# Twelve query feature maps by two ScalarE passes, three groups of spread reciprocals copied out of PSUM, and new instruction orders

## The chip, the cores and the metric

The kernel runs on one core of one Trainium2 chip. The metric is the device time of one execution in microseconds (us). A core has five engines, each with its own queue of instructions worked off in order: TensorE (PE in the profile; PEld is its weight load), VectorE (DVE), ScalarE (ACT), GpSimd (POOL) and SyncE (SP, which here issues DMAs). They are tied together by semaphores alone. TensorE writes to PSUM, which has eight banks; VectorE and ScalarE read it.

## The reference

Four residual layers on one sequence of 2,048 tokens and 512 features, in the order A, B, A, B with the same weights for both A layers and for both B layers. Each has 32 heads of 16 features. A is linear attention, B is attention in a sliding window of 256 keys.

```python
# layer A, after a layer norm of x (without gain or bias)
phi = lambda t: jnp.where(t > 0, t + 1, jnp.exp(t)) + 1e-6
pq, pk = phi(q), phi(k)
kv = jnp.einsum("bhsd,bhse->bhde", pk, v)
z = jnp.einsum("bhsd->bhd", pk)
num = jnp.einsum("bhqd,bhde->bhqe", pq, kv)
den = jnp.einsum("bhqd,bhd->bhq", pq, z)[..., None] + 1e-6
o = num / den                                 # then o @ wo, added to x

# layer B, after a layer norm of x
scores = jnp.einsum("bhqd,bhkd->bhqk", q, k) * (Dh ** -0.5)
mask = (idx[:, None] - idx[None, :] >= 0) & (idx[:, None] - idx[None, :] < 256)
p = _softmax(jnp.where(mask, scores, -1e9))
o = jnp.einsum("bhqk,bhkd->bhqd", p, v)       # then o @ wo, added to x
```

## The kernel before, in words

The sequence is cut into 16 tiles of 128 tokens. Everything stays in on-chip memory; x is loaded once and the result written once.

The program is not written engine by engine. `Plan` records every operation as a node of a graph, with its engine or a choice of engines, what it reads and writes and which PSUM banks it needs. A compressed table at the end of the file (`TABLE`) then gives three things: the order of all operations, the engine of each operation that has a choice, and the PSUM bank of each tile. `place` reads the table, `synchronise` derives the waits on semaphores, and each engine plays its operations in the table's order. So the table decides which instruction stands behind which on every engine.

The work has these stages. The first A layer: for each tile a layer norm (`norm`: statistics on VectorE, the inverse root on GpSimd, the scaling on VectorE), a transpose, the key product (`a_k`) with its feature map, the Gram sums of normed x against mapped keys ("g", line 475, 128 x 512 matmuls in four banks), and the query product (`a_q`, `feat`, line 414) with its feature map.

The feature map is `phi`. ScalarE takes the exponential out of PSUM into a buffer tE (line 423), VectorE clamps it to 1 and adds 1e-6 (line 424), and VectorE takes the maximum of that and the product in PSUM plus 1 + 1e-6 (line 425).

Then comes a barrier (`barrier`, lines 517 to 557), since linear attention needs the sums over all keys: kv is masked to blocks and multiplied into the output weights, giving M (four 512-column matmuls, line 521, each copied out of PSUM, "Me", line 389). For each group of four tiles the denominators are made on TensorE ("den", line 537), inverted by VectorE in float32 (line 541), cast to bf16 by either engine ("recb", line 542) and spread over the head features by TensorE into four banks ("spread", line 550). VectorE multiplies the mapped queries by each bank (line 557). Tiles of later groups pass the barrier later, inside the next stage.

The B layer (`middle`): for each tile the output of the A layer (`a_out`, added to x on line 568), a layer norm, query, key and value products (`b_qkv`, `b_v`), and then, for a block of 128 queries at a time, scores (`b_scores`, line 634), their exponentials on ScalarE (line 644), the causal mask on VectorE (line 652), scores and exponentials of the far end of the window (`b_far`, lines 723 and 732) with a mask on GpSimd or VectorE (lines 703 and 704), the product with the values (`b_values`, line 753), the division (lines 765 and 766) and the output product and residual (`b_out`). Keys are copied from PSUM ("bke", lines 585 and 586) and then put in a layout with zeros by two DMAs for each tile ("kd", on SP's queue); values likewise ("bve", "vd").

While the first B layer runs, the key products, value products ("ve", line 389) and some query products of the second A layer are already made for the tiles that are finished. The second barrier and the second B layer follow. In the two B layers ScalarE's exponentials of scores run nearly without a break; I call these the exponential stages.

Beside TensorE's own work there are 10 + 6 matmuls without use ("fill", lines 270 and 275).

## Time and profile before

| | |
|---|---|
| median of 3 runs | 412.48 us (412.22 to 414.48) |
| the profiled execution's own time | 412.48 us |
| its span, first to last instruction | 410.8 us |
| mean granted TensorE clock | 0.998 |
| busy: TensorE, VectorE, ScalarE, GpSimd | 389.5, 344.4, 341.9, 126.3 us |
| first exponential of scores of the first B layer | 62.75 us |
| first exponential of scores of the second B layer | 259.02 us |

Times inside the profile are microseconds from the start of the span. A group of instructions is given as line, engine, operation, output from input, shapes and count, then its busy time and the mean nanoseconds of one, then the engine's idle time just before them and what ended it. "idle before <- X" is a wait that X ended. The chain of waits is followed back from the last instruction: each piece is what the next one waited for, or the instruction before it on its engine. A stretch in which the chain stays on one engine is a stretch in which that engine did not wait.

### The profile page before, as it was taken

The numbers are of one execution on the slowest core, as the hardware profiler recorded it, in microseconds if no ns is written. First come the engines' busy times: TensorE is split into PE (matmuls) and PEld (weight loads), VectorE is DVE, ScalarE is ACT, GpSimd is POOL, SyncE is SP. The second block draws the span as 40 slices with busy tenths as digits, with TensorE's granted clock in tenths as the row PEclk, the third lists the DMA queues.
The fourth block names the chain that finished last, engine by engine and source line by source line (L and its number), as shares of the span: only waits on it lengthen the run. The fifth ranks groups of instructions, "written<-read, shape, count | busy, mean of one in ns | idle before, by whom it ended". The sixth has DMA issues, their size and how long they took to land.

```text
span 410.8 us, 17457 instructions
## 1 busy us (share of the span) xinstructions
PE 389.5 (95%) x7639; PEld 260.5 (63%) x7715; DVE 344.4 (84%) x803; ACT 341.9 (83%) x428; POOL 126.3 (31%) x221
## 2 busy tenths in 40 slices
PE   8999999999999999999999999999999989899996
PEld 4645676766475576565566767586757745566674
DVE  5998899989989899778887879997899778766675
ACT  2633559998999999999998255999999999999992
POOL 3665761122251253231401113112234024431310
PEclk9999999999999999999999999999999999999999
DMA  7934117542234624343212100443324333352442
GB/s 246 240 66 96 61 41 146 141 123 56 67 82 98 117 77 95 83 118 83 69 44 53 29 2 14 106 122 81 93 67 104 87 80 94 81 147 67 135 115 61
DMA packets 67460, 37.84 MB, mean 92 GB/s; under 512 B 48248, under 2 KB 62456, under 8 KB 67384
## 3 DMA queue, kind: packets, MB, share of 16 engines
q1 hardware_dynamic: 66896, 35.41, 35.6%
q8 instruction: 61, 1.00, 1.0%
q0 software_dynamic: 480, 1.31, 1.0%
q14 instruction: 15, 0.12, 0.1%
q10 hardware_dynamic: 8, 0.00, 0.0%
HBM read 6.29 MB, written 2.10 MB: 20 GB/s over the span
## 4 chain that ended last, share of the span: by engine, by line
PE 60%; ACT 26%; DVE 10%; issue 2%; DMA 1%; POOL 0%; DVEq 0%; POOLq 0%; SPq 0%
PE ps L400 21%; ACT pb L644 16%; PE ps L414 14%; PE ps L753 8%; PE ps L634 5%; ACT pb L732 4%; PE ps L475 3%; ACT vp L644 3%; DVE XQ L557 2%; ACT tE L423 1%; PE ps L723 1%; DVE xres L568 1%; DMA kB<-vp 1%; PE ps L1007 1%; PE ps L451 1%
## 5 line engine op out<-in xcount | busy, mean ns | idle before, releaser
L644 ACT ACTIVATE pb<-ps 128x1024 bf16<-128x1024 f32 (+2 forms) x224 | 206.8, 1022 | 6.3 <-PE ps L634 5.2
L753 PEld LDWEIGHTS ps<-vB,pb 128*128 128x128 bf16 x2560 | 77.7, 96 | 12.9 <-issue 3.7
L753 PE MATMUL ps<-vB,pb 128*128 128x34 bf16 x2560 | 83.8, 177 | 0.6 <-ACT pb L644 0.4
L414 PE MATMUL ps<-xT,wBp 128*128 128x128 bf16 x1024 | 69.1, 219 | 0.7 <-DVE stats L361 0.4
L423 ACT ACTIVATE tE<-ps 128x512 bf16<-128x512 f32 x64 | 38.4, 613 | 34.4 <-PE ps L400 14.7
L414 PEld LDWEIGHTS ps<-xT,wBp 128*128 128x128 bf16 x1024 | 59.1, 98 | 12.2 <-issue 4.4
L703 POOL TENSOR_SCALAR_AFFINE_SELECT pb<-pb 128x1024 bf16<-128x1024 bf16 x33 | 37.8, 1145 | 82.6 <-ACT pb L732 30.1
L363 POOL TENSOR_SCALAR ve<-mv 128x1 f32<-128x1 f32 x64 | 15.6, 243 | 142.6 <-DVE mv L362 140.3
L634 PE MATMUL ps<-XQ,kB 32*128 32x256 bf16 (+2 forms) x1024 | 49.6, 268 | 3.3 <-ACT vp L644 0.9
L568 DVE TENSOR_TENSOR xres<-ps,xres 128x512 bf16<-128x512 f32 x63 | 43.1, 684 | 8.8 <-PE ps L400 8.2
L400 PE MATMUL ps<-wA,XQ 128*128 128x512 bf16 x172 | 45.8, 379 | 2.1 <-issue 1.0
L361 DVE BATCH_NORM_STATS2 stats<-xres 128x6 f32<-128x512 bf16 x64 | 43.4, 682 | 2.4 <-DMA xres<-in_A_x_dram 2.0
L652 DVE TENSOR_TENSOR pb<-pb,tri 128x512 bf16<-128x512 bf16 (+1 forms) x112 | 43.2, 398 | 2.2 <-ACT pb L644 2.1
L732 ACT ACTIVATE pb<-ps 128x1024 bf16<-128x1024 f32 x42 | 41.5, 1065 | 0.6 <-PE ps L723 0.4
L364 POOL TENSOR_TENSOR rs<-ve,negh 128x1 f32<-128x1 f32 x64 | 36.9, 577 | 5.3
L414 PE MATMUL ps<-XQ,wA 128*128 128x128 bf16 x512 | 35.5, 219 | 0.0
L634 PEld LDWEIGHTS ps<-XQ,kB 32*128 32x128 bf16 x1024 | 15.5, 92 | 31.5 <-ACT pb L644 7.5
L414 PEld LDWEIGHTS ps<-XQ,wA 128*128 128x128 bf16 x512 | 30.7, 98 | 6.0 <-ACT pb L644 0.8
L400 PE MATMUL ps<-M,XQ 128*128 128x512 bf16 x113 | 30.9, 380 | 2.6 <-issue 1.0
L400 PE MATMUL ps<-wBv,xT 128*128 128x512 bf16 x111 | 31.1, 380 | 1.9 <-issue 1.1
L400 PE MATMUL ps<-wBo,oT 128*128 128x512 bf16 x107 | 29.7, 380 | 2.0 <-issue 0.6
L644 ACT ACTIVATE vp<-ps 128x1024 bf16<-128x1024 f32 (+2 forms) x32 | 26.6, 925 | 1.8 <-PE ps L634 1.8
(115 smaller groups left out, 530.6 us busy)
## 6 DMA issues: line engine op xcount, KB each, us to landing
vB<-vS SPq DMA_DIRECT2D x64, 136.0 KB, 2.6
kB<-vp SPq DMA_DIRECT2D x64, 128.0 KB, 2.1
wA<-in_A_wqkv_dram SPq DMA_DIRECT2D x3, 512.0 KB, 6.1
out_dram<-xres POOLq DMA_DIRECT2D x10, 128.0 KB, 2.1
xres<-in_A_x_dram SPq DMA_DIRECT2D x2, 512.0 KB, 5.2
pb<-in_B_wqkv_dram SPq DMA_DIRECT2D x1, 1024.0 KB, 7.1
xres<-in_A_x_dram SPq DMA_DIRECT2D x3, 256.0 KB, 5.0
out_dram<-xres SPq DMA_DIRECT2D x5, 128.0 KB, 2.2
```

The lines of the kernel that those rows point to most:

```text
L361: self.on("DVE", "stats", lambda e: e.bn_stats(K.stats[:, t, :], K.xres[:, t, :]), key, dve(512), rd=[("xres", t)], wr=[("stats", t)])
L364: self.pow = self.on("POOL", "pow", lambda e: e.tensor_tensor(K.rs[:, t, :], K.ve[:, t, :], K.negh[:], ALU.pow), key + 0.03, (640, 690), r ...
L400: m = e.matmul(K.ps(ps), lhs(c), rhs(c), start=c == 0, stop=c == 3)
L414: m = e.matmul(K.ps(ps)[:, f * P:(f + 1) * P], w(c, f), xT(c), start=c == 0, stop=c == 3)
L423: self.on("ACT", "E", lambda e: e.activation(K.tE[:, s, :], K.ps(ps), ACT.Exp, bias=0.0), key, act(512), wr=[("tE", s)], ps=[ps])
L568: self.on("DVE", "res", lambda e: e.tensor_tensor(K.xres[:, t, :], K.ps(po), K.xres[:, t, :], ALU.add), key, dve(512), rd=[("xres", t)], w ...
L634: m = e.matmul(K.ps(ps[gq])[:, ns * i:ns * i + ns], K.kB[rows, j % 4, 2 * f + b, :, :], K.XQ[rows, f, q:q + ns], start=True, stop=True, ti ...
L644: return e.activation(out(2 * h, 2, ns), i, ACT.Exp, bias=0.0, scale=0.25)
L652: return e.tensor_tensor(x, x, K.tri[:, 0, sh:64].unsqueeze(1).unsqueeze(1).to_broadcast([P, 4, n, 64 - sh]), ALU.mult)
L703: return e.affine_select(out=x, in_=x, compare_op=ALU.is_ge, fill=0.0, base=-2, pattern=[[0, 16], [-2, 64]], channel_multiplier=1)
L732: return e.activation(far(h), i, ACT.Exp, bias=0.0, scale=0.25)
L753: m = e.matmul(K.ps(ps)[:, 34 * u:34 * u + 34], K.P((b // 2) % rp)[:, gq, f, o:o + P], K.vB[:, (b // 2) % 4, b % 2, r, :], start=i == 0, s ...
```

## The change

Seven query tiles of the first A layer (0 to 6) and five of the second (4 to 8) get another form of the last step of the feature map: ScalarE reads the product out of PSUM a second time and writes it, plus 1 + 1e-6, in bf16 to the place of the mapped query; VectorE then takes the maximum of two bf16 tiles in on-chip memory, in place of the maximum that reads PSUM. For group 0 in the first barrier and groups 0 and 1 in the second, the spread reciprocals are first copied out of PSUM in bf16, by ScalarE or VectorE as the table says, into tE, and VectorE multiplies two bf16 tiles. The reciprocal is written in bf16 directly, and the cast "recb" is gone. The keys of tile 0 are written from PSUM straight into kB by two copies with a factor of 0 or 1 for each row (`par2`, made by a small reduction), and the copy and the two DMAs of that tile are gone. The first scores of each B layer are cut by query tile: `b_first` makes the 128 x 128 scores of query tile 0, then of tile 1, in place of two `b_scores` of 256 queries for two head groups each. The paths under `whole` and `po` are in the code but are switched off (`WHOLE` is empty and `FIRST` 0). The table is new: all orders, engine choices and banks.

By the orders of the two programs, ScalarE has seven of the copies of spread reciprocals and VectorE five. Of the operations with a choice some others change engine: M copies 8 and 0 (ScalarE, VectorE) to 6 and 2; value products 8 and 8 to 2 and 14; vS copies 7 and 25 to 9 and 23; key copies 8 and 24 to 5 and 25. Two far masks go from GpSimd to VectorE.

```diff
 LONG = ("mf", "zero", "wp", "c6", "c9", "c10", "c14", "c21", "c24")
-SHORT = ("xn", "mk", "md", "ma", "mf", "E1", "recb")
+SHORT = ("xn", "mk", "md", "ma", "mf", "E1", "mx", "pm")
...
+WHOLE = {2: (), 3: ()}
+FIRST = {2: 0, 3: 0}
+BY_ACT = {2: (0, 1, 2, 3, 4, 5, 6), 3: (4, 5, 6, 7, 8)}
+COPIED = {2: (0,), 3: (0, 1)}
+PART = (2, 3)
+NEAR = (0,)
...
+        pool("c2c", zero(lambda: K.one, 1.0 + 1e-6), key + 2, 100, wr=[("one",)])
...
+        self.on("DVE", "par", lambda e: e.tensor_reduce(K.par2[:], K.ident[:].rearrange("p (n a) -> p a n", a=2), mybir.AxisListType.X, ALU.add), 150, dve(128), rd=[("ident",)], wr=[("par",)], after=after)
...
-    def phi(self, ps, out, wr, key, ring):
+    def phi(self, ps, out, wr, key, ring, near=False):
...
         self.on("ACT", "E", lambda e: e.activation(K.tE[:, s, :], K.ps(ps), ACT.Exp, bias=0.0), key, act(512), wr=[("tE", s)], ps=[ps])
+        if near:
+            self.on("ACT", "R", lambda e: e.activation(out(), view(K.ps(ps)), ACT.Identity, bias=K.one[:]), key + 0.005, act(512), rd=[("one",)], wr=wr, ps=[ps])
         self.on("DVE", "E1", lambda e: e.tensor_scalar(K.tE[:, s, :], K.tE[:, s, :], 1.0, 1e-6, op0=ALU.min, op1=ALU.add), key + 0.01, dve(512, "4x"), rd=[("tE", s)], wr=[("tE", s)])
-        self.on("DVE", "phi", lambda e: e.scalar_tensor_tensor(out(), K.ps(ps) if len(out().shape) == 2 else K.ps(ps).rearrange("p (f n) -> p f n", f=4), 1.0 + 1e-6, K.tE[:, s, :] if len(out().shape) == 2 else K.tE[:, s, :].rearrange("p (f n) -> p f n", f=4), ALU.add, ALU.max), key + 0.02, dve(512), rd=[("tE", s)], wr=wr, ps=[ps])
+        if near:
+            self.on("DVE", "mx", lambda e: e.tensor_tensor(out(), out(), view(K.tE[:, s, :]), ALU.max), key + 0.02, dve(512, "2x"), rd=[("tE", s)], wr=wr)
+        else:
+            self.on("DVE", "phi", lambda e: e.scalar_tensor_tensor(out(), view(K.ps(ps)), 1.0 + 1e-6, view(K.tE[:, s, :]), ALU.add, ALU.max), key + 0.02, dve(512), rd=[("tE", s)], wr=wr, ps=[ps])
...
-            self.on("DVE", "rec", lambda e, G=G, ps=ps: e.reciprocal(K.recf[:], K.ps(ps)[:, 0:P]), k + 0.1, dve(128, "recip"), wr=[("recf",)], ps=[ps])
-            self.g.add("recb", {"ACT": act(128), "DVE": dve(128, "2x")}, lambda e, eng, G=G: e.activation(K.rec[:, G, :], K.recf[:], ACT.Copy) if eng == "ACT" else e.tensor_copy(K.rec[:, G, :], K.recf[:]), k + 0.1, rd=[("recf",)], wr=[("rec", G)])
+            def inverse(e, G=G, ps=ps):
+                with K.nc.allow_low_precision(reason="one rounding, to the type that the product reads"):
+                    return e.reciprocal(K.rec[:, G, :], K.ps(ps)[:, 0:P])
+
+            self.on("DVE", "rec", inverse, k + 0.1, dve(128, "recip"), wr=[("rec", G)], ps=[ps])
...
+                if G in COPIED[ph + 1]:
+                    sl = tg % 2
+                    self.copy("sc", bc[tg], lambda sl=sl: K.tE[:, sl, :], lambda b=bc[tg]: K.ps(b), k + 0.25 + 0.01 * tg, 512, wr=[("tE", sl)])
+                    self.on("DVE", "pm", lambda e, x=x, sl=sl: e.tensor_tensor(x(), K.tE[:, sl, :].rearrange("p (f n) -> p f n", f=4), x(), ALU.mult), k + 0.3 + 0.01 * tg, dve(512, "2x"), rd=[("XQ", t), ("tE", sl)], wr=[("XQ", t)])
+                    continue
                 self.on("DVE", "pqd", lambda e, x=x, b=bc[tg]: e.tensor_tensor(x(), K.ps(b).rearrange("p (f n) -> p f n", f=4), x(), ALU.mult), k + 0.3 + 0.01 * tg, dve(512), rd=[("XQ", t)], wr=[("XQ", t)], ps=[bc[tg]])
...
+        if t in NEAR:
+            for a in range(2):
+                o, i = lambda a=a: K.kB[:, r, :, :, a], lambda: K.ps(pk).rearrange("p (b n) -> p b n", b=8)
+                self.either("kz", lambda e, eng, a=a, o=o, i=i: e.activation(o(), i(), ACT.Copy, scale=K.par2[:, a:a + 1]) if eng == "ACT" else
+                            e.tensor_scalar(o(), i(), K.par2[:, a:a + 1], None, op0=ALU.mult), key + 0.05, 512, rd=[("par",)], wr=[("kB", r, a)], ps=[pk])
+            return
...
+    def b_first(self, p, key):
...
+        ps = [Tile(1, "S") for _ in range(4)]
+
+        def put(e):
+            m = None
+            for f in range(4):
+                for gq in range(4):
+                    rows = slice(32 * gq, 32 * gq + 32)
+                    m = e.matmul(K.ps(ps[gq])[:, P * f:P * f + P], K.kB[rows, 0, 2 * f, :, :], K.XQ[rows, f, P * p:P * p + P], start=True, stop=True, tile_position=(32 * gq, 0))
+            return m
+
+        self.pe("s", put, key, 1, 512, mode=(32, 128), occ=237, rd=[("kB", 0, 0), ("kB", 0, 1), ("XQ", p)], ps=ps)
+        for h in range(2):
...
+            self.on("ACT", "ex", ex, key + 0.01 * h, act(1024), wr=[("P", 0, f, 0, h + 3 * p) for f in range(4)], rd=[("P", 0, f) for f in range(4)], ps=two)
+        if p == 0:
+            x = lambda: bass_view(K.P(0)[:, 0, 0, 0:64], [[704, 16], [1, 64]])
+            self.on("DVE", "md", lambda e: e.tensor_tensor(x(), x(), K.tri[:, 0, :].unsqueeze(1).to_broadcast([P, 16, 64]), ALU.mult), key + 0.02, dve(1024, "2x"),
+                    rd=[("P", 0, f, 0, h) for f in range(4) for h in range(2)] + [("tri",)], wr=[("P", 0, f, 0, 2) for f in range(4)])
...
-                    if f % wide[b] == 0:
+                    if j + b == 0 and ph in PART:
+                        if f < 2:
+                            self.b_first(f, base + 0.25 * f)
+                    elif f % wide[b] == 0:
                         self.b_scores(j, b, list(range(f, f + wide[b])), base + j + (f + b) / 4)
```

More of the change, by code (lines that the diff above doesn't have):

```diff
@@ L366, in norm @@
         self.transpose("T", xn, out, [name], wr, key + 0.05, by_pe)
+        if po:
+            self.copy("xe", po, lambda: K.xres[:, t, :], lambda: K.ps(po), key + 0.06, 512, wr=[("xres", t)])
     def transpose(self, name, src, out, rd, wr, key, by_pe):
@@ L389, in copy, with tok @@
         return self.either(name, lambda e, eng: e.activation(out(), src(), ACT.Copy) if eng == "ACT" else e.tensor_copy(out(), src()), key, n, rd=rd, wr=wr, ps=[ps])
-    def tok(self, name, t, lhs, rhs, rd, key):
+    def tok(self, name, t, lhs, rhs, rd, key, whole=False):
         K = self
         ps = Tile(1, K.cls)
+        if whole:
+            self.pe("id", lambda e: e.matmul(K.ps(ps), K.ident[:], K.xres[:, t, :], start=True, stop=False), key - 0.01, 1, 512, rd=[("xres", t), ("ident",)], ps=[ps])
         for h in range(2):
@@ L399, in put @@
                 for c in (2 * h, 2 * h + 1):
-                    m = e.matmul(K.ps(ps), lhs(c), rhs(c), start=c == 0, stop=c == 3)
+                    m = e.matmul(K.ps(ps), lhs(c), rhs(c), start=c == 0 and not whole, stop=c == 3)
                 return m
@@ L757, in b_values @@
                 rd += [("P", i % K.rp, f)] + [("vB", i % 4, a, b) for a in range(2) for b in range(2)]
-                rd += [("P", i % K.rp, f, b, h_) for h_ in range(3) for b in (0, 1)]
+                rd += [("P", i % K.rp, f, b, h_) for h_ in range(5) for b in (0, 1)]
             rd += [("A", i % K.rp) for i in range(max(0, j - 2), j + 1)]
@@ L769, in b_values, with b_out @@
             key + 0.03, dve(256), rd=[("rc", s, h)], wr=[("o", s, h)], ps=[ps])
-    def b_out(self, j, key, by_pe):
+    def b_out(self, j, key, by_pe, whole=False):
         K = self
@@ L865, in middle @@
                 continue
-            self.b_out(j, k, tail)
+            po = self.b_out(j, k, tail, j in WHOLE[ph])
             if last:
```

158 lines of the change are left out of this document (88 added, 70 removed).

## The prediction

> **What bounds the kernel now.** I read the page's busy shares and chain first, then the busy time of each engine by stage, then the chain of waits inside the two stretches in which ScalarE is not full, and last the groups and ScalarE's own timeline. Page first.
>
> ```profile
> PE 389.5 (95%) x7639; PEld 260.5 (63%) x7715; DVE 344.4 (84%) x803; ACT 341.9 (83%) x428; POOL 126.3 (31%) x221
> PE 60%; ACT 26%; DVE 10%; issue 2%; DMA 1%; POOL 0%; DVEq 0%; POOLq 0%; SPq 0%
> ```
>
> Three engines are almost equally loaded, so the mean tells little. The span falls into five stages: up to the first exponential of scores, the first exponential stage, the stretch between the two, the second exponential stage, the end. The first five rows below are those stages; the last two are the barriers, from the last sums over the keys to the next scores. Columns: stretch and its length, then busy us (and count) of PE, PEld, DVE, ACT, POOL, then clock, DMA share, GB/s.
>
> ```profile
> 0.00:62.70 62.70, 60.68 (x595) 35.83 (x605) 54.17 (x132) 28.02 (x48) 38.30 (x82) 1.00 0.48 125
> 62.70:225.50 162.80, 156.85 (x3234) 104.47 (x3272) 142.03 (x331) 156.71 (x187) 42.93 (x71) 1.00 0.40 91
> 225.50:259.00 33.50, 32.48 (x511) 24.34 (x517) 28.97 (x67) 16.28 (x29) 7.01 (x13) 1.00 0.10 27
> 259.00:403.50 144.50, 135.88 (x3242) 93.56 (x3263) 115.38 (x266) 140.88 (x166) 38.03 (x55) 1.00 0.38 96
> 403.50:410.80 7.30, 3.60 (x72) 2.32 (x69) 3.89 (x11) 0.00 (x0) 0.00 (x0) 0.88 0.24 67
> 45.10:62.70 17.60, 17.23 (x245) 12.43 (x250) 17.19 (x36) 10.02 (x18) 11.21 (x20) 1.00 0.12 32
> 243.10:259.00 15.90, 15.30 (x237) 11.61 (x240) 15.70 (x35) 9.67 (x17) 3.89 (x8) 1.00 0.10 37
> ```
>
> The reader is to see this: in the exponential stages ScalarE is the bound (156.71 of 162.80 and 140.88 of 144.50 us); outside them it is half idle. In the two barriers VectorE is as full as TensorE (17.19 against 17.23 of 17.60, 15.70 against 15.30 of 15.90). The change takes work from VectorE there; what that is worth hangs on TensorE, which keeps its work. So I look at how much TensorE waits.
>
> ```profile
> 8.01 1.73 PE ps L400 x8
> 9.73 0.89 PE ps L414 x16
> 31.11 0.38 PE ps L498 x16
> 40.63 0.39 PE ps L400
> 41.04 0.60 ACT tE L423
> 41.67 0.37 DVE tE L424
> 42.06 0.70 DVE vp L425
> 42.81 0.60 PE ps L475 x2
> 224.12 0.22 PE ps L634 x8
> 243.10 1.09 ACT M L389 x2
> 244.20 0.14 issue
> 244.33 0.41 PE ps L550 x16
> 258.49 0.33 PE ps L634 x8
> ```
>
> A 512-column matmul costs 1.73/8 = 0.216 us, a 128-column one 0.89/16 = 0.056 us. TensorE follows on itself except at two places: 41.02 to 42.81, where the last key feature map (exponential, clamp, maximum) holds up the Gram sums, 1.8 us; and 243.10 to 244.33, where two copies of M stand in front of the spread, 1.2 us.
>
> **The change part by part.** I count against the profiled execution: its span is 410.8 us and its own time 412.48 us, 1.7 us around the span. That time is also the median of the runs shown, so nothing is carried over. A measurement of this kernel can tell about 0.5%, 2.1 us, from no change.
>
> ```profile
> L423 ACT ACTIVATE tE<-ps 128x512 bf16<-128x512 f32 x64 | 38.4, 613 | 34.4 <-PE ps L400 14.7 <-DVE XQ L425 8.2 <-PE ps L414 7.4
> L425 DVE SCALAR_TENSOR_TENSOR XQ<-ps,tE 128x512 bf16<-128x512 f32 x32 | 21.8, 682 | 0.2
> L557 DVE TENSOR_TENSOR XQ<-ps,XQ 128x512 bf16<-128x512 f32 x32 | 20.6, 681 | 1.8 <-PE ps L550 1.6
> L652 DVE TENSOR_TENSOR pb<-pb,tri 128x512 bf16<-128x512 bf16 (+1 forms) x112 | 43.2, 398 | 2.2 <-ACT pb L644 2.1
> L389 DVE CAST vS<-ps 128x512 bf16<-128x512 f32 x25 | 17.2, 688 | 4.3 <-PE ps L400 3.9
> L389 ACT ACTIVATE vS<-ps 128x512 bf16<-128x512 f32 x7 | 4.8, 686 | 0.6 <-PE ps L400 0.6
> L389 ACT ACTIVATE vp<-ps 128x512 bf16<-128x512 f32 x8 | 4.8, 612 | 0.2 <-PE ps L400 0.2
> L585 ACT ACTIVATE vp<-ps 128x512 bf16<-128x512 f32 x8 | 6.3, 784 | 0.8 <-PE ps L414 0.8
> L389 ACT ACTIVATE XQ<-ps 128x512 bf16<-128x512 f32 x7 | 4.2, 601 | 0.9 <-PE ps L414 0.6
> kB<-vp SPq DMA_DIRECT2D x64, 128.0 KB, 2.1
> ```
>
> Feature map of twelve tiles. Each loses a 0.682 us VectorE pass that reads PSUM and gets a ScalarE pass and a VectorE maximum of two bf16 tiles. The trace has no such maximum; its nearest row is the mask product, 0.398 us for the same 512 columns. VectorE: 12 x (0.398 - 0.682) = -3.4 us; if the maximum ran no faster than from PSUM, 0.0. ScalarE: 12 x 0.613 = +7.4 us (between 0.601 and 0.784 a pass). By the order of the changed program all twelve lie ahead of the first exponentials of their stage, seven in the first stage, five in the third, where ScalarE has 34.7 and 17.2 us unused. I cost them at nothing on the path; the cover is that idle time. The Trainium skill (ScalarE: Activation LUTs, What ACT_TABLE_LOAD costs) says a bias read from a [128,1] operand adds about 93 ns to an ACTIVATE; that would be 12 x 0.093 = 1.1 us, an estimate from the page, in the same idle time, so the sum stays.
>
> Spread copied out for three groups, twelve tiles. The order gives seven copies to ScalarE (one in the first barrier, six in the second) and five to VectorE. VectorE per tile: -0.681 + 0.398, and +0.688 where it copies. First barrier: 3 x 0.688 + 4 x (0.398 - 0.681) = +0.9 us; second: 2 x 0.688 + 8 x (0.398 - 0.681) = -0.9. ScalarE: 7 x 0.61 = +4.3 us, outside the exponential stages again. No gain on the path for either; the loss, if the first barrier's VectorE is the one that ends last, is the 0.9. Here a page speaks against the change: the Trainium skill (VectorE: DVE Perf Modes, Rules for kernel authors) says to take the PSUM read at single rate, or to copy out first "if you'll do many ops"; one op follows here.
>
> The reciprocal written in bf16 drops eight casts of some 0.3 us and one link between reciprocal and spread; I give it nothing, since in the first barrier TensorE has other work there.
>
> Keys of tile 0 written straight into kB: two ScalarE passes in place of one copy and two DMAs on SP's queue, which move up the rest of it. The chain to the first scores loses about 2.1 us of DMA and gains one pass of 0.78 at most, twice. But at 258.49 the scores followed TensorE's own work, not the DMA: nothing on the path. The first two score blocks are cut by tile instead of by head pair; the same four exponentials of 1,024 columns remain, one 1,024-column mask replaces two of 512. The constants (one memset, one small reduction) lie at the start beside other work: at most one 0.7 us VectorE pass, at about 35 us, where VectorE has room.
>
> The new orders, which I take to decide the time. Four terms.
>
> First stage. Up to the first scores TensorE has 596 matmuls of the same kinds in both programs. In the new order 14 Gram matmuls and 32 one-column sums stand between the last key products and the two Gram matmuls that need the last feature map: 14 x 0.216 + 2 x 0.38 = 3.8 us over a chain of 1.7 us. The wait goes: -1.75 us. What is late next is VectorE, which must deliver the earlier maps in time. Bounds: -1.8 and 0.
>
> First exponential stage, ScalarE's own work. Beside the exponentials the old order has 30 passes there, the new one 28: one feature exponential more (+0.613), two vS copies more (+1.372), one key copy less (-0.784), four value copies less (-2.448): -1.25 us. VectorE gets about 2 us more there and has 20.8 free. Bounds: -1.25 and, should VectorE's extra copies hold up TensorE, +0.8.
>
> The end of that stage:
>
> ```profile
> 220.71 1.08 ACT L644 ACTIVATE pb<-ps 128x512 bf16<-128x512 f32 x2
> 222.32 0.66 ACT L644 ACTIVATE pb<-ps 128x256 bf16<-128x256 f32 x2 [0.52 <-PE ps L634]
> 224.40 1.08 ACT L644 ACTIVATE pb<-ps 128x512 bf16<-128x512 f32 x2 [1.42 <-PE ps L634]
> ```
>
> ScalarE waits 1.94 us for the last scores, behind TensorE's query products. In the new order 1.76 us of matmuls (16 of 128 columns, 4 of 512) stand over two passes of 1.08, and then 0.89 us of matmuls over 0.66 us of passes and a feature exponential: a wait of 0.7. Gain -1.2 us; bounds -1.9 and 0.
>
> Between the stages. From the last scores at 224.12 to the next at 258.49 are 34.4 us. The new order has six 512-column matmuls more there (four key or value products, two of the layer's output): 6 x 0.216 = +1.3 us. Two of the four M copies go to VectorE, and query products stand between M and the spread, so the 1.2 us wait at 243.10 should go: about 0 together; bounds -1.2 and +1.3.
>
> Second exponential stage: one XQ copy more on ScalarE, +0.6 us. The end is left as it is.
>
> Sum: -1.75 - 1.25 - 1.2 + 0 + 0.6 = -3.6 us, so 408.9 us. All terms at their good ends give -1.8 - 1.25 - 1.9 - 1.2 + 0.6 = -5.6 (406.9), at their bad ends 0 + 0.8 + 0 + 1.3 + 0.6 = +2.7 (415.2).
>
> **Rivals.** No change: TensorE's waits move and do not go. The Gram matmuls wait for earlier maps, the ramp down and the M copies cost what they did; only the counted work is left: -1.25 + 1.3 + 0.6 = +0.65, 413.1 us. For it: VectorE, which feeds all of them, gains nothing over the whole kernel by my count. Against: it is relieved where it is full.
>
> Slower: ScalarE becomes the bound of the second barrier. There it had 17 passes; from its first M copy to the first exponential the new order has 25. If the 8 x 0.61 = 4.9 us all fall behind waits, the 6.2 us it sat idle there stay and the exponentials start 4.9 us later. It decides once ScalarE's waits there exceed 15.9 - 9.67 - 4.9 = 1.3 us. With the counted work and without the first stage's wait: 412.5 + 4.9 + 0.65 - 1.75 = 416.3 us. For it: the key passes stand behind copies that wait for the spread. Against: those waits were for TensorE and VectorE, and VectorE is relieved.
>
> More gain: the waits inside the first exponential stage, 162.80 - 156.71 = 6.1 us with the 1.94 counted above, shrink also. Two thirds of the other 4.2 would be 2.8: 406.1 us. Nothing in the order shows it clearly.
>
> Copying out does not pay: the first barrier's VectorE, 17.19 of 17.60 us full, gets the 0.9 us and holds up the scores: 408.9 + 0.9 = 409.8 us. For it: the fullness. Against: the casts gone and the one tile's cheaper map. It is that page's rule as a mechanism of this kernel.
>
> **How the numbers follow.** Chances: the forecast 0.42 (408.9, its own range 407.0 to 410.4), copying does not pay 0.07, more gain 0.15, no change 0.22, slower 0.14. Faster by over 0.5% means below 410.4: the forecast, more gain and most of the copying case, 0.62. Within 0.5% is the no-change case with what is left, 0.24. Slower, above 414.5: 0.14. The range runs from just below the more-gain case to the upper edge of the no-change case and a little over, 405.5 to 414.8; the slower case is left out.
>
> **What would show it.** After the last key product TensorE should run on with no wait over 0.5 us; the first exponential should come near 61 us. ScalarE's busy time should be near 350 us (341.9 plus some 8.5), in the first exponential stage some 155. The maximum and the product from the copied tile should last near 0.4 us, the added ScalarE pass 0.6 to 0.8. From the last scores of one stage to the first of the next should be 34 to 35 us. I am wrong if the first exponential is no earlier, if ScalarE is full ahead of the second exponential stage, or if waits for scores inside the exponential stages grow.

## The result, and the profile after

The changed kernel is slower: 416.37 us median against 412.63 us, a ratio of 1.0056 with a 95% interval of 1.003 to 1.0083. The ratio goes with the means, 415.73 and 413.40 us without the one slow run of 419.48 us, so the loss is 2.3 us and not the 3.7 between the medians. The forecast was 408.9 us with a range of 405.5 to 414.8. The profiled execution took 416.38 us with a span of 414.7 us.

The rows below are the stages of the kernel after, in the columns of the stage rows above: stretch and length, then busy us (and count) of TensorE, weight load, VectorE, ScalarE, GpSimd, then clock, DMA share, GB/s.

```profile
PE 389.4 (94%) x7671; PEld 261.6 (63%) x7747; DVE 348.3 (84%) x809; ACT 349.7 (84%) x441; POOL 127.3 (31%) x219
0.00:64.50 64.50, 61.30 (x603) 36.24 (x613) 54.17 (x136) 32.24 (x55) 38.43 (x82) 1.00 0.49 117
64.50:226.10 161.60, 155.92 (x3240) 104.43 (x3276) 144.55 (x330) 155.61 (x184) 44.17 (x71) 1.00 0.43 91
226.10:260.30 34.20, 33.62 (x518) 24.70 (x526) 30.59 (x72) 19.91 (x37) 7.63 (x15) 1.00 0.09 18
260.30:405.90 145.60, 134.64 (x3233) 93.52 (x3255) 114.90 (x263) 141.56 (x166) 37.11 (x52) 1.00 0.44 95
405.90:414.70 8.80, 3.94 (x86) 2.75 (x83) 4.11 (x10) 0.41 (x2) 0.00 (x0) 0.93 0.22 60
```

The reader is to see that the engines did the work that was forecast: ScalarE's busy time is 349.7 us (forecast 350) and 155.61 us in the first exponential stage (forecast 155). It bought no time. Against before, the first exponential comes 1.8 us later, its stage is 1.1 us shorter, and the three stretches behind it are 0.6, 1.4 and 1.2 us longer: 3.9 us in sum, more than the 2.3 us of the means, since these are two single executions. TensorE is as busy as before (389.4 against 389.5 us), so the 3.9 us are idle time of TensorE. VectorE, which the change was to relieve, has not become emptier: 54.17 us in the first stage before and after, 30.59 against 28.97 between the stages.

Next the chain of waits of the kernel after, in order of time: start, length, what the chain was on.

```profile
12.94 6.75 DMA XQ<-vp
41.07 3.02 PE ps L500 x14
44.09 0.78 PE ps L523 x32
252.52 0.61 ACT tE L443
253.15 0.69 ACT XQ L445
253.84 0.74 ACT kB L623
254.60 0.83 ACT kB L623
255.43 0.45 ACT xT L401
404.63 4.30 DMA oT<-o
```

Three places are new. A transpose of the layer-normed tiles on SP's queue takes 6.75 us to come through (4.50 in before). In the second barrier the chain runs over ScalarE through the added pass (line 445) and the two key copies (line 623); TensorE's own timeline shows no wait of over 0.15 us there. At the end stands a transpose of the attention output of 4.3 us. The wait in front of the Gram sums is gone as forecast: they run on without a break from 41.07 us.

The added instructions, by groups of the kernel after (busy us, mean ns, idle us before them):

```profile
L443 ACT ACTIVATE tE<-ps 128x512 bf16<-128x512 f32 x64 | 37.9, 611 | 24.0 <-PE ps L419 16.2 <-DVE vp L450 3.3 <-DVE XQ L448 3.0
L445 ACT ACTIVATE XQ<-ps,one 128x512 bf16<-128x512 f32 x12 | 8.4, 697 | 0.2
L448 DVE TENSOR_TENSOR XQ<-XQ,tE 128x512 bf16<-128x512 bf16 x12 | 4.9, 429 | 0.0
L588 DVE TENSOR_TENSOR XQ<-tE,XQ 128x512 bf16<-128x512 bf16 x12 | 4.8, 418 | 0.2
L406 DVE CAST tE<-ps 128x512 bf16<-128x512 f32 x5 | 3.4, 686 | 0.1
```

The maximum and the product from bf16 tiles last 0.43 and 0.42 us (forecast 0.4). The added pass lasts 0.70 us where the exponential of the same shape lasts 0.61: the 86 ns fit the some 93 ns that the Trainium skill (ScalarE: Activation LUTs, What ACT_TABLE_LOAD costs) gives for each [128,1] operand, here the bias.

### The profile page after: what moved, and what is told of

It reads as the page before. It is cut to its first block, busy times and chain, and to the rows that moved or that the text cites. A ratio compares the mean times of both kernels' runs of the same rounds, so it can differ in the third digit from the quotient of the medians.

```text
span 414.7 us, 17531 instructions
## 1 busy us (share of the span) xinstructions
PE 389.4 (94%) x7671; PEld 261.6 (63%) x7747; DVE 348.3 (84%) x809; ACT 349.7 (84%) x441; POOL 127.3 (31%) x219
## 4 chain that ended last, share of the span: by engine, by line
PE 60%; ACT 22%; DVE 10%; issue 3%; DMA 3%; POOL 1%; POOLq 0%
PE ps L419 20%; PE ps L433 13%; ACT pb L685 12%; PE ps L821 11%; PE ps L675 6%; ACT vp L685 4%; PE ps L500 3%; ACT pb L800 2%; DMA XQ<-vp 2%; ACT tE L443 1%; DVE xres L603 1%; PE ps L791 1%; DVE vS L406 1%; DVE pb L693 1%; DMA oT<-o 1%
## 5 line engine op out<-in xcount | busy, mean ns | idle before, releaser
L685 ACT ACTIVATE pb<-ps 128x1024 bf16<-128x1024 f32 (+2 forms) x216 | 199.1, 1024 | 5.9 <-PE ps L675 5.3
L378 POOL TENSOR_SCALAR ve<-mv 128x1 f32<-128x1 f32 x64 | 17.0, 265 | 154.5 <-DVE mv L374 152.2
L771 POOL TENSOR_SCALAR_AFFINE_SELECT pb<-pb 128x1024 bf16<-128x1024 bf16 x32 | 36.6, 1145 | 79.0 <-DVE pb L772 33.9
L675 PE MATMUL ps<-XQ,kB 32*128 32x256 bf16 (+3 forms) x992 | 48.0, 267 | 4.7 <-DVE o L834 0.7
L419 PE MATMUL ps<-wA,XQ 128*128 128x512 bf16 x177 | 46.7, 379 | 2.8 <-DMA XQ<-vp 1.0
L379 POOL TENSOR_TENSOR rs<-ve,negh 128x1 f32<-128x1 f32 x64 | 38.9, 608 | 5.3
L833 DVE RECIPROCAL rc<-ps 128x16 f32<-128x16 f32 x64 | 16.3, 254 | 15.2 <-PE ps L821 14.7
```

The lines of the kernel that those rows point to most:

```text
L379: self.pow = self.on("POOL", "pow", lambda e: e.tensor_tensor(K.rs[:, t, :], K.ve[:, t, :], K.negh[:], ALU.pow), key + 0.03, (640, 690), r ...
L419: m = e.matmul(K.ps(ps), lhs(c), rhs(c), start=c == 0 and not whole, stop=c == 3)
L675: m = e.matmul(K.ps(ps[gq])[:, ns * i:ns * i + ns], K.kB[rows, j % 4, 2 * f + b, :, :], K.XQ[rows, f, q:q + ns], start=True, stop=True, ti ...
L685: return e.activation(out(2 * h, 2, ns), i, ACT.Exp, bias=0.0, scale=0.25)
L771: return e.affine_select(out=x, in_=x, compare_op=ALU.is_ge, fill=0.0, base=-2, pattern=[[0, 16], [-2, 64]], channel_multiplier=1)
```

## The experiments

The table holds the stages of each profiled execution in us, and the ratio to the kernel before with its 95% interval. "End of the first stage" is the end of the last exponential of the first exponential stage; "end" counts from the last exponential of all to the span as the page prints it, so it holds to 0.05 us. One execution's second stage alone is no evidence below some 4 us: with the order of before untouched it read between 144.0 and 147.6. In three of the long ones, e10, e11 and e15, the granted TensorE clock was half for 3.4, 3.4 and 6.8 us of that stage (see the last section).

| kernel | first exponential | end of the first stage | between | second stage | end | ratio |
|---|---|---|---|---|---|---|
| before | 62.75 | 225.48 | 33.54 | 144.17 | 7.61 | 1 |
| after | 64.53 | 226.14 | 34.16 | 145.62 | 8.78 | 1.0056 |
| e16: after again | 66.93 | 228.52 | 34.15 | 143.78 | 8.75 | 1.0035 (1.0007 to 1.0063) |
| e3: after, wAo late | 63.99 | 225.60 | 34.16 | 143.98 | 8.76 | 1.0013 (0.9991 to 1.0035) |
| e17: the same again | 63.22 | 225.18 | 34.15 | 144.40 | 9.07 | 1.0026 (0.9997 to 1.0054) |
| e11: before, wAo early | 62.99 | 225.45 | 33.53 | 145.02 | 7.60 | 1.0019 (0.9998 to 1.0039) |
| e10: old order, neither form | 63.13 | 225.75 | 33.41 | 147.63 | 7.61 | 1.0001 (0.9968 to 1.0035) |
| e8: old order, maximum only | 63.70 | 225.98 | 34.42 | 144.41 | 7.59 | 1.0055 (1.0028 to 1.0082) |
| e9: old order, copies only | 63.98 | 226.22 | 35.56 | 144.22 | 7.60 | 1.0082 (1.0058 to 1.0106) |
| e1: old order, both forms | 64.79 | 227.81 | 36.62 | 144.22 | 7.55 | 1.0138 (1.0104 to 1.0173) |
| e14: before, more TensorE | 62.66 | 227.51 | 33.54 | 144.01 | 7.64 | 1.0058 (1.0026 to 1.0091) |
| e15: before, less ScalarE | 62.75 | 227.80 | 33.74 | 148.47 | 7.59 | 1.0036 (1.0007 to 1.0065) |

### Forms or orders: both forms in the old order (e1), old operations in the new order (e2, e4)

My first theory was that the forms are harmless and the new orders cost the time. e1 keeps the order and banks of before and adds both forms (the keys of tile 0 and the first scores are made as before); e2 keeps the order of after and takes both forms out; e4 takes them out in the second barrier alone.

```diff
 e1
-NEAR = (0,)
-PART = (2, 3)
+NEAR = ()
+PART = ()
 TABLE: order, engines and banks of before; the added pass stands right behind its
 exponential, each copy right ahead of its product
 e2
-BY_ACT = {2: (0, 1, 2, 3, 4, 5, 6), 3: (4, 5, 6, 7, 8)}
-COPIED = {2: (0,), 3: (0, 1)}
+BY_ACT = {2: (), 3: ()}
+COPIED = {2: (), 3: ()}
 e4
+BY_ACT = {2: (0, 1, 2, 3, 4, 5, 6), 3: ()}
+COPIED = {2: (0,), 3: ()}
```

> The kernel before with the two forms alone (twelve query maps by two ScalarE passes and a bf16 maximum, twelve spread tiles copied out first with the engines of the changed kernel, the reciprocal in bf16 without its cast), in the old orders and banks; keys of tile 0 and the first scores as before. Theory 1, the new orders cost the time: 410.5 to 413 us, no slower than before. Theory 2, the added ScalarE passes cost it: 415 to 417 us.

> The changed kernel with both forms undone (feature map by one ScalarE pass and a VectorE maximum out of PSUM, spread multiplied straight out of PSUM), in the new orders; where a bank was freed by the ScalarE pass, clamp and maximum stand earlier on VectorE, and 53 of 1,013 banks are others. Theory 1: 415 us or more, since the orders stay and lose their relief. Theory 2: 412 to 413.5 us.

> The changed kernel with both forms undone in the second barrier alone (five query maps, eight spread tiles); 35 banks are others. If ScalarE, 14.1 of 16.2 us full ahead of the second exponential stage, is the bound there, the first exponential of that stage comes 0.7 us or more earlier: 415.7 us or less. If the two forms help VectorE there, it comes later: 417 us or more.

e1 took 418.41 us, 1.4% over before. The exponential stages kept their lengths (163.02 and 144.22 us); the first stage grew by 2.0 us and the stretch between by 3.1. So in the old order the forms by themselves cost time in the very places where I had costed them at nothing, and the theory that the orders alone cost it fell.

e2 took 430.37 us (1.0416, 1.0388 to 1.0443) and e4 427.9 us (1.0357, 1.033 to 1.0383). In e4 the stretch between grew to 37.09 us and the second exponential stage to 153.34 us (3.4 of them at half the clock), though no operation of that stage was touched: 20 of the 35 PSUM banks that had to change lie in it. The two show that the new order and its banks fit no other set of operations; what the forms are worth in it they do not tell.

### Which form: the maximum alone (e8), the copies alone (e9), neither (e10), all in the old order

```diff
 as e1, and
 e8:  COPIED = {2: (), 3: ()}
 e9:  BY_ACT = {2: (), 3: ()}
 e10: both of these
 TABLE: order, engines and banks of before
```

> The orders and PSUM banks of the kernel before, with the bf16 maximum for the twelve tiles and no copying (the separate cast of the reciprocals is gone as in the change). Theory: it is the second ScalarE pass behind the exponential that holds up the copies of M and of the features behind it on ScalarE's queue, so most of the 5 us by which the two forms together lengthened the old order are here: about 416.5, with the second barrier near 36 us. Rival: the copies do it; then this kernel is at 413.5 and the second barrier at 33.8.

> The orders and PSUM banks of the kernel before, with the spread reciprocals of the three groups copied out of PSUM and no maximum form. Theory: about 414.5, some 1.0 us of the 5 us of both forms together, since three of four copies in the first barrier are on VectorE, which has no idle time there. Rival, that the copies carry the cost of the second barrier: 416.5 with the second barrier near 36 us.

> The orders and banks of the kernel before with neither form: only the bf16 reciprocal without its cast and the two constants (one memset, one reduction) are left of the change. If the 1.0 to 1.2 us by which the first exponential came later with either form alone belong to the forms, this kernel has it at 62.8 us and takes 412.9; if they belong to what is left here, it has it at 63.7 and takes 413.9.

e10 is not told apart from before, so the bf16 reciprocal and the two constants cost nothing that can be measured. The maximum alone costs 0.55%, the copies alone 0.82%, both 1.38%: they add. I had expected most of it from the maximum; in the stretch between, the copies have 2.0 us of the 3.1 and the maximum 0.9. The chain of e9 there shows how:

```profile
243.84 1.09 ACT M L406 x2
244.94 0.60 ACT M L406
245.53 0.51 ACT tE L406
246.06 0.43 DVE XQ L588
246.49 0.61 DVE tE L406
247.13 0.43 DVE XQ L588
247.59 0.61 ACT tE L406
248.22 0.44 DVE XQ L588
```

The first copy stands on ScalarE behind the copies of M, and each product can begin only when its copy is done. A tile that VectorE copies itself takes 0.61 + 0.43 us. ScalarE is idle on the whole here, but not at the moment that counts, and TensorE waits for the third tile (timeline of e9; a matmul record is missing just ahead of it, and the same wait in e1, where none is, is 0.52 us):

```profile
248.93 0.38 PE L419 MATMUL ps<-M,XQ 128*128 128x512 bf16 x1 [0.71 <-DVE XQ L588]
```

Later in the same stretch it stands 0.31 and 0.65 us more for ScalarE's copies, at 259.6 and 261.3 us.

In before the three products come straight out of PSUM, 1.89/3 = 0.63 us each (VectorE's timeline):

```profile
244.79 1.89 DVE L557 TENSOR_TENSOR XQ<-ps,XQ 128x512 bf16<-128x512 f32 x3 [0.16 <-PE ps L550]
```

And the chain of before in the same stretch is TensorE's own from 244.33 on:

```profile
244.33 0.41 PE ps L550 x16
244.74 1.00 PE ps L414 x16
245.74 1.34 PE ps L400 x6
```

### The load of wAo: late again in the kernel after (e3, e17), early in the kernel before (e11), and the kernel after once more (e16)

Comparing the queues showed a step of the new order that the prediction does not have. SP's queue, before first, then after (start, us, instruction):

```profile
12.35 1.29 SPq L371 DMA_TRANSPOSE XQ<-vp  x1
38.43 0.50 SPq L290 DMA_DIRECT2D wAo<-in_A_wo_dram  x1
```

```profile
10.33 0.51 SPq L296 DMA_DIRECT2D wAo<-in_A_wo_dram  x1
12.94 1.31 SPq L388 DMA_TRANSPOSE XQ<-vp  x1
```

The weights wAo, needed at 47 us, are now loaded 28 us earlier, ahead of the first key transposes. e3 puts that one load back.

```diff
 SP's queue in the kernel after
-load of wAo
 transpose 5, load of half of wB, transposes 6 to 15, load of wBv
+load of wAo
```

> The changed kernel, with one thing moved on SyncE's queue: the 0.5 MB load of wAo stands behind the key transposes of the first stage, where it stood before, and not ahead of the first of them. If that load makes the first transposes land late (6.75 us for the first of them in the profile after) and TensorE wait for them, the first exponential comes 1 to 2 us earlier and the time is 414.5 to 415.4 us. If TensorE would be late there anyway, 416.4 us.

> The kernel before with one instruction moved: the load of wAo stands ahead of the key transposes on SP's queue, as in the change. If that step costs by itself, TensorE waits for the transposes near 20 us, the first exponential comes at about 63.5 and the time is about 414; if only the new orders have no room for it, both stay at 62.8 and 412.9.

> The kernel after, unchanged, beside the next one on the same chip. If the early load of wAo is the whole measurable loss, it is 1.5 to 2 us slower than the next kernel; if the gap between the two was partly between sessions, the two lie within 1 us.

> The kernel after with the load of wAo back behind the key transposes, as before, beside the kernel after: 414.2 if the first comparison held.

TensorE's timeline, in the kernel after, in e16 (the same kernel, another execution) and in e17 (load late), each with the idle time in front of the instruction and what ended it:

```profile
19.82 0.59 PE L419 MATMUL ps<-wA,XQ 128*128 128x512 bf16 x2 [1.04 <-DMA XQ<-vp]
```

```profile
20.76 0.59 PE L419 MATMUL ps<-wA,XQ 128*128 128x512 bf16 x2 [2.62 <-DMA XQ<-vp]
```

```profile
23.05 0.59 PE L419 MATMUL ps<-wA,XQ 128*128 128x512 bf16 x2 [0.46 <-DMA XQ<-vp]
```

With the early load TensorE stands 1.04 or 2.62 us, with the late one 0.46 (0.44 in e3), and the end of the first exponential stage follows: 226.14 and 228.52 against 225.60 and 225.18 us. Before had no such wait. In e16 the wait is not the whole of the delay: behind it the granted clock (the third figure from the right) was half for 3.4 us, which is up to 1.7 us of TensorE's work.

```profile
21.80:25.20 3.40, 3.40 (x9) 1.22 (x8) 1.08 (x4) 1.68 (x3) 0.48 (x2) 0.51 0.83 177
```

In time, e3 is no longer told apart from before (1.0013); e16 and e17, side by side, had medians of 415.32 and 414.38 us, 0.9 us apart (means 0.6 us), less than the 1.5 to 2 expected and not told apart. All the kernels of this order with the late load, e3, e5, e6, e13 and e17, have ratios between 0.9996 and 1.0026; the two measurements with the early one have 1.0056 and 1.0035. In the kernel before, the same move left the stages as they were up to the second exponential stage; TensorE waited 0.22 us for a transpose at 18.6 us, and the time is not told apart (1.0019, 0.9998 to 1.0039). So the early load costs little where it stands alone, and with the rest of the new order 0.1% (e16 and e17, side by side) to 0.4% (after and e3, measured apart).

### What sets the end of the first exponential stage: more TensorE work (e14), less ScalarE work (e15)

Leaving out the kernel after itself, the kernels with a form in the old order and e2 (230.27), that stage ended between 225.2 and 225.8 us in every kernel, wherever the first exponential lies and however many passes ScalarE has. TensorE's busy time up to there is the same too: 60.68 + 156.85 = 217.5 us before, 61.30 + 155.92 = 217.2 after. e14 makes half a key product twice for eight tiles inside the stage (the first result is overwritten). e15 gives ten of ScalarE's copies there to VectorE.

```diff
 e14, in tok
+                if more and h == 0:
+                    for c in (0, 1):
+                        e.matmul(K.ps(ps), lhs(c), rhs(c), start=c == 0, stop=c == 1)
                 for c in (2 * h, 2 * h + 1):
 e15, in TABLE
-engine of three bke, three bve, four ve: ACT
+engine of three bke, three bve, four ve: DVE
```

> The kernel before, in which the first two of the four matmuls of the key product are done twice for eight tiles inside the first exponential stage: sixteen 512-column matmuls more, 16 x 0.216 = 3.5 us of TensorE, nothing else. Theory: the end of the first exponential stage, which stood at 225.5 us in every kernel with unhindered transposes whatever came first, is set by TensorE's work up to there; it moves by 2.5 to 3.5 us and the time to about 415.5 to 416. Rival, the prediction's: ScalarE's passes set it; then TensorE's extra work fits beside them, the end moves by less than 1 us and the time stays under 414.

> The kernel before, with ten copies inside the first exponential stage (three of keys, three and four of values) done by VectorE in place of ScalarE; order and banks unchanged. ScalarE loses about 10 x 0.7 = 7 us there. Theory, TensorE sets the stage's end: it stays at 225.5 within 0.7 us, ScalarE only waits more, and the time stays within 1 us of 412.7. Rival, the prediction's, which gave 1.25 us for two passes less: the end moves forward by 4 to 7 us and the time to 406 to 409.

The first exponential stage of e14, then of e15, in the columns of the stage rows:

```profile
62.66:227.50 164.84, 159.94 (x3249) 106.00 (x3284) 142.50 (x331) 156.67 (x187) 42.92 (x71) 1.00 0.40 90
```

```profile
62.75:227.80 165.05, 157.15 (x3234) 104.44 (x3269) 146.74 (x340) 152.16 (x177) 42.83 (x71) 1.00 0.40 89
```

3.2 us more of TensorE (159.94 against 156.8) moved the end by 2.0 us with ScalarE's busy time unchanged, and the whole kernel by 0.58%. 4.5 us less of ScalarE (152.16 against 156.7) moved the end not forward but 2.3 us back, with VectorE 4.8 us busier. So passes moved from ScalarE to VectorE do not shorten this stage, though ScalarE is 96% busy, and work added to TensorE lengthens it. That e15 came later because VectorE, which feeds TensorE, got the copies is argued: no run took work off ScalarE alone.

The trace of e3 shows how full TensorE is. It has 7,747 matmuls on record where that of the kernel after, which makes the same ones, has 7,671; the 76 missing are all 512 columns wide, and their time looks like idle time. The same stage in e3:

```profile
64.00:225.60 161.60, 160.23 (x3276) 104.46 (x3275) 144.52 (x330) 155.64 (x184) 44.23 (x71) 1.00 0.42 92
```

TensorE is busy for 160.23 of 161.60 us, ScalarE for 155.64. In e1, in the old order and with every matmul on record too, TensorE has 161.01 of 163.02 us. So TensorE hardly waits in this stage, ScalarE waits 6 us, and with e14 TensorE is the bound.

### The first stage and the copies in it (e12, e6)

```diff
 e6, on e3
-COPIED = {2: (0,), 3: (0, 1)}
+COPIED = {2: (), 3: (0, 1)}
 e12
-BY_ACT = {2: (0, 1, 2, 3, 4, 5, 6), 3: (4, 5, 6, 7, 8)}
-COPIED = {2: (0,), 3: (0, 1)}
+BY_ACT = {2: (), 3: (4, 5, 6, 7, 8)}
+COPIED = {2: (), 3: (0, 1)}
 TABLE: up to the first scores that of before, then that of after
```

> The kernel after, with the load of wAo back behind the key transposes, and the four spread reciprocals of the first barrier multiplied straight out of PSUM again (3 of 1,013 PSUM banks change with it). If copying costs time in the first barrier, by the ScalarE pass and the three copies that VectorE itself makes there, the first exponential comes before 63.6 us and the time is about 413.5; if copying relieves VectorE as it was meant to, the first exponential comes at 64.5 or later and the time is about 414.8; if it does nothing, both stay (64.0 and 414.2).

> Up to the first scores the order, engines and banks of the kernel before, with neither form there; behind them the order of the change, with both forms in the second barrier and the keys of tile 0 written directly (2 of 1,005 banks differ). If the stages stand for themselves: first exponential at 62.9, exponential stage 161.7, between the stages 34.2, second stage 144.0, end 7.6 to 8.8: a time of 412.0 to 413.2. If the rest of the new order needs the state that its own first stage leaves, the exponential stage is 162.7 or more and the time above 413.5.

e6 took a ratio of 1.0011 (0.9981 to 1.0041), the first exponential at 63.78 and the stage's end at 225.49 us: in the new order the copies of the first barrier change nothing that can be measured. e12 fits neither expectation: 1.0031 (1.0006 to 1.0055), the first exponential at 64.05, the stage 161.56 us long and its end at 225.61. With the order of before in front, the first exponential still came 1.3 us later and the end of the stage not at all, so the first exponential is a poor mark of progress. Of the 1.3 us TensorE stands 0.57 us at 58.78 us for ScalarE's two key copies (line 623), 1.71 us long, which I had put at nothing on the path.

### The end: output stores moved (e5), VectorE's code shifted (e13)

In all kernels with the new order but e6 the stretch behind the last exponential is 8.8 to 9.1 us, in e6 and in all with the old order 7.6 to 7.7. The chain shows the last transpose of the attention output, 4.3 us, where it landed 2.4 us after its issue in before. e5 moves two output stores that stood on GpSimd's queue behind a mask ahead of it. e13 puts twelve one-column writes at the start of VectorE's program.

```diff
 e5, GpSimd's queue in e3
-store, mask, store, store
+store, store, store, mask
 e13, on e3, start of VectorE's program
+                    for i in range(12):
+                        e.memset(self.pad[:, i:i + 1], 0.0)
```

> The kernel after, with the load of wAo back behind the key transposes, and two of the last output stores on POOL's queue issued before the last triangular mask on POOL instead of behind it. Theory: the last transpose of the attention output lands late (4.3 us instead of 2.5) because two stores of 128 KB, held back on POOL's queue behind that mask, are issued 1.2 us before it; moved forward they are done by then. The stretch behind the last exponential falls from 8.8 to about 7.5 us and the time from 414.2 to about 412.9. Rival: the transpose is slow because of the two value loads ahead of it on SP's own queue; then the stretch stays at 8.8 and the time at 414.2.

> The kernel after with the load of wAo back behind the key transposes and twelve one-column writes to a buffer that nothing reads, at the start of VectorE's program while it waits for x. Nothing else differs, but the places at which VectorE's code is loaded lie twelve instructions earlier. Theory: the last transpose of the attention output lands 4.3 us after its issue, not 2.5, because a load of 16 KB of code falls into it; here that load comes some 4 us earlier, the transpose lands in 2.5 us and the stretch behind the last exponential is 7.6 us instead of 8.8; the time falls by up to 1.1 us to 413.1. Rival: it is the order of SP's queue; then the stretch stays at 8.8 and the time at 414.2.

e5 (1.0017, 0.9989 to 1.0046) has the stretch at 8.80 us and on its chain

```profile
402.60 4.37 DMA oT<-o
```

with both stores long done. The theory of the stores fell. So did its rival, since e6 has the same two value loads directly ahead on SP's queue and its transpose landed in 2.5 us. e13 (0.9996, 0.9969 to 1.0022) did not test what it was made for: a load of code still came at 404.43 us (404.29 in e3), 1.9 us after the transpose's issue in both, so it is hardly VectorE's; the stretch stayed at 8.88 us. What does tell the cases apart is told in the last section.

## Why the prediction was wrong

First stage, -1.75 us ("The wait goes: -1.75 us"): this step failed, and the trace of before could have told it. TensorE's timeline of before at that place:

```profile
40.84 1.03 PE L475 MATMUL ps<-vp 128*128 128x512 bf16 x4
41.71 0.54 PE L498 MATMUL ps<-ones,vp 128*128 128x1 bf16 x16
42.11 1.31 PE L475 MATMUL ps<-vp 128*128 128x512 bf16 x4
```

While the chain ran over ScalarE and VectorE from 41.02 to 42.81 us, TensorE did other matmuls. Four Gram matmuls took 1.31 us in place of 1.03: the wait was worth 0.28 us. The stage row said as much, 60.68 us busy of 62.70, and 1.25 of the 2.02 idle lie at the start, so 0.8 us was all there was to gain. The new order did remove the wait. In its place TensorE waited 1.04 us (2.62 in e16) for the key transposes, which the early load of wAo holds up; its idle time in the stage rose from 2.02 to 3.20 us. I never read the order of SP's queue. The sentence "What is late next is VectorE" named the wrong thing.

First exponential stage, -1.25 us from ScalarE's own passes: this step failed. The count was right (156.71 to 155.61 us) and worth no time; e15 took four times as much off ScalarE and the stage ended later. I read a 96% busy engine as the bound. TensorE had 156.85 us in the same row, and 160.23 of 161.60 us in e3, where all its matmuls are on record.

Ramp down, -1.2 us: failed for the same reason. The waits for the last scores did fall, from 1.94 to 0.95 us, but ScalarE's idle time in the whole stage went only from 6.1 to 6.0 us: its waits for TensorE moved to other places.

Between the stages, 0 (bounds -1.2 and +1.3): it was +0.6 us, inside the bounds. The work that I counted as more is there: TensorE is busy for 33.62 us against 32.48, and for 1.2 us less in the second exponential stage. The M-copy wait taken off was, like the Gram wait, smaller than the chain made it: the idle time in front of the spread was 0.17 us, and all idle time in the stretch fell from 1.02 to 0.58 us.

```profile
244.33 0.41 PE L550 MATMUL ps<-rec,spread 32*128 32x128 bf16 x16 [0.17 <-ACT M L389]
```

Second exponential stage, +0.6: ScalarE's busy time grew by 0.7 us as counted; the length, between 143.4 and 145.6 us in the kernels with this order, is not told apart from before. "The end is left as it is": +1.2 us.

The two forms at nothing on the path, covered by ScalarE's idle 34.7 and 17.2 us: failed as a price, for e8 and e9 put 0.55% and 0.82% on the old order, outside the exponential stages. The idle time is real but lies at other moments. In the new order their price is not known: e6 finds nothing for the copies of the first barrier, and e2 and e4, which take forms out, changed the fit of order and banks as well. The chain over ScalarE from 252.52 to 255.88 us is no price either, since TensorE works on meanwhile.

The rivals. "Copying out does not pay" had the right mechanism for the old order, at a price too small: in e9 TensorE stands 0.75 us for VectorE in the first barrier (line 380, at 55.67 us), as that rival says, and the second costs 2.0 us more. In the new order e6 does not find it. The rule of the Trainium skill (VectorE: DVE Perf Modes, Rules for kernel authors), to copy out first only for many operations, agrees with these 0.61 + 0.43 us against 0.63. "No change" came nearest in what holds it: waits that move and do not go. What I set against it, that VectorE "is relieved where it is full", did not come: it has 15.75 of 16.20 us in the second barrier, after 15.70 of 15.90. "Slower" gave 416.3 us, and 416.4 came, but that is luck and not its mechanism: the stretch with the second barrier became 0.6 us longer, not 4.9, although ScalarE's waits there, 16.20 - 14.13 = 2.1 us, had passed its point of 1.3.

```profile
244.10:260.30 16.20, 15.87 (x246) 11.90 (x249) 15.75 (x39) 14.13 (x26) 4.49 (x9) 1.00 0.05 18
```

What adds up to the loss: 0.7 us at the end of the first exponential stage (3.0 in e16, half clock included), 0.6 between, 1.2 at the end, 2.5 together against 2.3 between the means (1.7 for e16). That the load makes TensorE wait is shown by moving it; that it costs the 0.1 to 0.4% is likely and not shown. The 0.6 is the matmuls that moved there, by the rows. The 1.2 is the late last transpose; what makes that late stays open. The last two appear in nearly every kernel with the new order and in none with the old operations and order. No kernel here beat before; e10 and e13 are not told apart from it.

## What to carry to other kernels

A stretch of the chain of waits on another engine is not idle time of the engine that follows: read that engine's own timeline for what it did meanwhile, and cap any gain by its idle time in the stage. Before calling a busy engine the bound of a stage, see whether all its instructions are on record, add or remove a few us on each candidate and see what the end of the stage does; here the engine that I took for the bound did not set it. When an order is made anew, compare every queue's order, that of the DMA issuer too, and count an engine's idle time as cover only at the moments when the work falls due.

## What the runs showed of the hardware

DMA transposes landed later where code was loaded while they ran. Below, the DMA packets around the last transpose: first e6, in the 2.5 us from its issue and then in the 0.8 us behind them; second the kernel after, in the 2.1 us from its issue and in the 1.6 us behind them. Queue q8 loads instructions, q1 carries the transpose, q0 an output store.

```profile
q0 software_dynamic: 89, 0.23, 28.0%
q1 hardware_dynamic: 546, 0.13, 26.1%
...
q8 instruction: 1, 0.02, 7.5%
```

```profile
q0 software_dynamic: 89, 0.23, 33.6%
q1 hardware_dynamic: 541, 0.13, 31.3%
q8 instruction: 1, 0.02, 4.2%
...
q1 hardware_dynamic: 3, 0.00, 0.2%
```

In e6 all packets of the transpose are through before the 16 KB of code come. In the kernel after the code comes among them, and the last three packets follow up to 1.6 us behind the others (541 + 3 = 544, as many as the same transpose has in before). In nine of the 18 profiles the load began 1.8 to 2.5 us after the issue of that transpose, and it landed in 4.3 to 4.6 us; in the other nine it began 2.3 to 3.0 us after it, and it landed in 2.4 to 2.5; between 2.3 and 2.5 us both are seen. Over the 142 transposes behind 55 us in the profiles of before and after whose landing is on record, 46 had a load on q8 begin within 2.4 us of the issue, and 31 of these took over 3.5 us; of the other 96 two did (4.5 us at most), with a median of 2.5. The Trainium skill (Runtime: NRT & Kernel Launch, Instruction fetch mechanics) says that crossing a 16 KiB block is mostly hidden. That speaks of the engine that runs the code; here another queue's transpose landed about 2 us later. It is a match in time and not a proof: no run moved the load by itself.

Long waits of TensorE went with a halved clock. In e10 a transpose in the second exponential stage landed 4.52 us after its issue, with a load on q8 begun 2.15 us after it, and TensorE stood:

```profile
367.36 1.04 PE L433 MATMUL ps<-xT,wBp 128*128 128x128 bf16 x8 [2.19 <-DMA xT<-xn]
```

From 367.2 us on the granted clock was half for 3.4 us. In e15 a transpose of the same kind took 4.62 us, TensorE stood 2.26 us, and the clock was half for 6.8 us; in e16 the 2.62 us at the key transposes were followed by 3.4 us. No other wait behind the first 5 us was over 2 us, but e4 and e11 had 3.4 us of half clock beside waits of 0.5 to 0.8 us, so the wait alone is not shown to be the cause.
